# Hash attention and a maxout FFN on one core: sets of four heads placed by GpSimd instead of by transfers, with a new plan

## The chip, the cores and the metric

The kernel runs on one core of one Trainium2 chip. The metric is the device time of one execution in microseconds, the median of three runs. Engines: TensorE (PE for matmuls, PEld for its weight loads), VectorE (DVE), ScalarE (ACT), GpSimd (POOL), SyncE (SP, which here only issues DMAs). "A unit" is a step of the kernel's outer loop, explained below; it is the kernel's own clock.

## The reference

q, k and v have 4 batches of 8 heads of 768 tokens of 64 numbers; proj is 64x6. Each token falls in one of 64 buckets by the signs of six projections, and a query sees only keys of its own bucket:

```
q_bucket = sum((q @ proj > 0) * 2**arange(6));  k_bucket likewise
scores = where(q_bucket == k_bucket, q @ k.T / 8, -1e9)
attn = exp(scores - max) / (sum + 1e-9);  x = attn @ v      # heads side by side: 3072 x 512
h = max(x @ w1, x @ w2, x @ w3)                             # 512 -> 768
out = h @ w_out                                             # 768 -> 512, float32
```

## The kernel before, in words

**Masking by extra rows.** A head's S tile holds the 64 transposed numbers of its tokens (scaled, bf16) and under them six or eight rows of bits as +-0.5. The scores matmul over these 70 or 72 rows gives the scaled score plus a term that is at its maximum only where all bits agree; the exponential on ACT (L387) with its bias leaves the rest at almost nothing. No mask is ever formed.

**Units.** A unit is two blocks of 128 keys against one half (384) of a head's queries: two matmuls (L385) into PSUM, one exponential over 128x768 into one of the AT tiles (L387). There are 192 units; batch 0 is units 0 to 47 and takes heads two by two: pair 0 in units 0 to 11, pair 1 in 12 to 23, then the set of heads 4 to 7 in 24 to 47. Every later batch takes 48 units, 24 for each half of the queries.

**Getting S.** The heads come in three ways. Pair 0 and pair 1 are transposed by PE (L198), copied out of PSUM (L210), and GpSimd scales them into S (L217). Their bits come from PE hashes; for pair 0 VectorE writes them in place (L264), for pair 1 it writes a tile (L241) that SP's DMAs carry into S (L245). All other heads come in *sets* of four, one set for q and one for k for each g from 1 to 7, called q1, k1, ... q7, k7 here. `load_quad` (L277) loads one head into each 32 partitions, a DMA for each head. `turn` (L288) transposes 32x32 blocks on VectorE, four instructions a set. `narrow` (L295) scales to bf16 on GpSimd, two instructions a set, and `place` (L302) moves each head with a DMA on SP's queue to partitions 0 to 63 of the set's S tile. `quad_hash` (L312) and `quad_bits` (L318) make the bits of both sets of a g, and four DMAs on SP (L324) take them to S.

**The rest.** `values` (L431) multiplies AT with v for four heads at once, 24 matmuls a pass; `sums` (L445) adds up AT with a matmul of ones, for which, from unit 48 on (`adds`), VectorE first adds the AT tiles of a head (`gather`, three instructions a head: L413, L416, L418). `inverse` and `spread` (L452 to L460) turn sums into factors, `scale` (L464) writes the scaled result to the xT tiles. The FFN takes a half batch as 24 items: 18 groups of four matmuls (L545), of which ACT copies one and VectorE takes the maximum with two others (L551), then six items of the output matmul (L561). From unit 40 on one FFN item runs in each unit.

**Order.** Every engine executes in the order in which the program issues to it. Each step has a due time in units in PLAN; steps are sorted by it and issued when the loop passes it, which sets the order on each engine and on the DMA queues (SP, ACT, and GpSimd's own). A step with a negative time, or one whose time is earlier than the loop has reached, is issued as soon as it is seen, in order of those times. For g of 4 and more the times are offsets from the unit at which that g is first used. A step waits on its engine for its data and for free buffers: five load tiles (`nat`), three turned tiles (`t32`), 26 AT tiles.

The steps of the plan that come up below: `t` turns, `pl` placing, `l` loads of sets, `w` the eight half weights and `v` the values on GpSimd's queue, `p1t`/`p1k`/`p1h`/`p1b` transposes, copies, hashes and bits of pair 1, `h` hashes of sets, `q0` to `q6` and `q` the sums, values and scaling, `act` the copies that ACT makes, `last` the end.

Of the kernel before, what the change touches and what calls it, by code (L numbers as in the profile page):

```python
# [17 lines left out]
def kernel(  # L18
# [21 lines left out]
    Q = 32  # L40
# [11 lines left out]
    NAT = 26  # L52
# [31 lines left out]
        'adds': 48,  # L84
        'act': [(1, 0, 0), (3, 0, 1), (2, 1, 1), (2, 1, 0), (3, 1, 0), (1, 1, 1)],
        'last': ['F', 'A00', 'S', 'I', 'A10', 'A01', 'R0', 'R1', 'A11', 'X01', 'X10', 'X00', 'X11'],
        'ffn': [40, 53, 10],
        'skip': [],
        't1': [-45.57, -44.264, -44.181, -35.522],
        'pl1': -31.678,  # L90
        't0': [-37.547, -33.595, -26.867, -24.071],
        'pl0': -20.267,
        'l1': [-58.53, -72.053, -70.663, -68.669],
        'l0': [-59.075, -55.548, -56.26, -58.067],
        'vl': -20.089,
        'h': [-23.27, -23.26],
        'q': {'S': 0.71, 'I': 0.71, 'A00': 0.711, 'R0': 0.721, 'X00': 0.722, 'A01': 0.725, 'X01': 7.804, 'A10': 0.576, 'R1': 0.746, 'X10': 3.72, 'A11': 0.743, 'X11': 0.988},
        'fill': [8, 0, 0],
# [5 lines left out]
    t16_pool = ctx.enter_context(tc.tile_pool(name="t16", bufs=3))  # L104
# [8 lines left out]
    x_pool = ctx.enter_context(tc.tile_pool(name="xpool", bufs=3))  # L113
# [72 lines left out]

    def load_pair(pi, eng, sides=(1, 0), h0=0, h1=2):
# [48 lines left out]
    def pair_bits(pi, hds):  # L236
# [6 lines left out]
        for hd, side, n in gs:  # L243
            done.update(("bits", pi, 2 * side + hd, par) for par in range(2))
            nc.sync.dma_start(s_at(pi, 2 * side + hd, D, D + NBITS, 0, S).rearrange("b (c n) -> b c n", c=2),  # L245
# [23 lines left out]
    def load_quad(side, g, xs, eng):  # L269
        if (side, g) not in nat:  # L270
            start_set((side, g), [(side, 4 * g + x) for x in range(4)])
        for x in xs:
            done.add(("load", side, g, x))
            b, h = divmod(4 * g + x, H)
            src = (q, k)[side][b, h].rearrange("(cc t m) d -> t cc (m d)", cc=CC, t=Q)
            dst = nat[side, g][x * Q : (x + 1) * Q, :].rearrange("t (cc w) -> t cc w", cc=CC)
            eng.dma_start(dst, src)  # L277

    def turn(name, u, half):
        assert all(("load",) + name + (x,) in done for x in range(4))  # L280
# [9 lines left out]
    def narrow(name, u):  # L290
        if name not in t16:
            t16[name] = t16_pool.tile([P, 2, S], BF16, tag="T16", name="T16")
        assert {("turn", name, u, half) for half in range(2)} <= done
        done.add(("narrow", name, u))
        nc.gpsimd.tensor_scalar(out=t16[name][:, u, :], in0=t32[name][:, u, :], scalar1=RS, scalar2=1.0,  # L295
                                op0=AluOp.mult, op1=AluOp.mult)

    def place(name, xs):
        assert {("narrow", name, u) for u in range(2)} <= done
        for x in xs:  # L300
            done.update(("place", name, x, par) for par in range(2))
            nc.sync.dma_start(s_tile(name)[0:D, x, :], t16[name][x * Q : (x + 1) * Q, :, :])  # L302
# [486 lines left out]
```

## Time and profile before

| what | value |
|---|---|
| median of 3 runs | 273.28 us (270.22 to 274.68) |
| the profiled execution | 275.35 us, span 273.4 us |
| mean granted TensorE clock | 0.967 |
| PE busy | 256.5 us, 94% |
| VectorE busy | 196.4 us, 72% |
| ScalarE busy | 181.3 us, 66% |
| GpSimd busy | 62.8 us, 23% |
| moved by DMA | 31.76 MB, 22658 packets |

The span runs from the first to the last instruction of the profiled execution; all times in the views count from its start. Views that are used: the page's rows of busy tenths in 40 slices; the busy time of each engine in chosen stretches; the chain that ended last, followed back from the last instruction; the waits of an engine with what ended them; groups of instructions by line (line, engine, operation, out<-in, count, busy us, mean ns, idle before); and the timeline of single instructions (start, length, engine, line, and in brackets the idle time before it with what ended it).

### The profile page before, as it was taken

Reading aid. Unit: us, or ns where it says so; the run is one execution under the profiler, and the core shown is the slowest. Engines: PE = TensorE matmul, PEld = TensorE weight load, DVE = VectorE, ACT = ScalarE, POOL = GpSimd, SP = SyncE. Lnnn points to the kernel's source line nnn. Section 1 sums busy time; section 2 is a strip of 40 time slices with the busy share of each in tenths; the row PEclk is TensorE's granted clock in tenths of the full one; section 3 lists DMA queues with packets and bytes.
Section 4 is the critical chain, followed back from the end, with each engine's and each line's share of the span. In section 5 each row is a group of like instructions: output and inputs, shape, how many; then the busy total and the mean of one; then the engine's idle time right before and its main releaser. Section 6 shows DMA issues by size and latency. Waiting matters only on the chain.

```text
span 273.4 us, 5808 instructions
## 1 busy us (share of the span) xinstructions
PE 256.5 (94%) x2198; PEld 139.4 (51%) x2198; DVE 196.4 (72%) x450; ACT 181.3 (66%) x273; POOL 62.8 (23%) x102
## 2 busy tenths in 40 slices
PE   8864769999999999999999999999999999999995
PEld 4411223355555555555555555555555555555563
DVE  2753535675599789988898889987967887695350
ACT  3683374778399919993799648991999399911422
POOL 4275243913213332063016102202000000000000
PEclk9995895999999999999999999999999999999999
DMA  7999999899622732573356406324221001100303
GB/s 227 227 218 212 250 184 260 197 181 159 155 67 90 226 90 72 98 230 95 94 80 211 109 14 113 121 56 64 71 79 38 2 0 52 65 2 0 117 0 115
DMA packets 22658, 31.76 MB, mean 116 GB/s; under 512 B 2872, under 2 KB 18152, under 8 KB 22632
## 3 DMA queue, kind: packets, MB, share of 16 engines
q0 software_dynamic: 8704, 12.59, 24.5%
q1 hardware_dynamic: 13496, 18.30, 24.1%
q10 hardware_dynamic: 432, 0.52, 0.6%
q8 instruction: 17, 0.28, 0.4%
q14 instruction: 9, 0.07, 0.1%
HBM read 25.17 MB, written 6.29 MB: 115 GB/s over the span
## 4 chain that ended last, share of the span: by engine, by line
PE 80%; DMA 15%; SPq 2%; DVE 1%; issue 0%; POOL 0%; ACTq 0%; ACT 0%; DVEq 0%
PE ms L545 34%; PE sc L385 19%; PE ms L431 11%; PE ms L561 11%; DMA nat<-in_q_dram 8%; DMA S<-T 4%; PE ms L312 3%; DMA nat<-in_k_dram 3%; PE ms L445 2%; SPq L324 1%; PE ms L572 0%; SPq L302 0%; SPq L277 0%; POOL T L295 0%; DVE xT L464 0%
## 5 line engine op out<-in xcount | busy, mean ns | idle before, releaser
L387 ACT ACTIVATE AT<-sc 128x768 f16<-128x768 f32 x192 | 154.0, 828 | 62.3 <-PE sc L385 56.2
L545 PE MATMUL ms<-xT,w_sb 128*128 128x384 f16 x576 | 112.9, 326 | 0.4 <-DVE ht L551 0.4
L385 PE MATMUL sc<-S 72*128 72x384 bf16 (+1 forms) x360 | 88.7, 336 | 9.6 <-DMA S<-bits 7.0
L545 PEld LDWEIGHTS <-w_sb 128*128 128x128 f16 x576 | 55.9, 97 | 38.8 <-issue 0.9
L551 DVE TENSOR_TENSOR ht<-ht,ms 128x384 f16<-128x384 f16 x96 | 52.6, 547 | 27.2 <-PE ms L545 24.3
L385 PEld LDWEIGHTS <-S 72*128 72x128 bf16 (+1 forms) x384 | 36.4, 100 | 49.0 <-issue 21.5
L295 POOL TENSOR_SCALAR T<-T 128x768 bf16<-128x768 f32 x28 | 24.2, 864 | 113.4 <-DVE T L288 69.2
L431 PE MATMUL ms<-AT,vo 128*32 128x385 f16 (+1 forms) x768 | 36.4, 331 | 0.0
L561 PE MATMUL ms<-wout_sb,ht 128*128 128x512 f16 x138 | 36.0, 378 | 0.0
L549 ACT CAST ht<-ms 128x384 f16<-128x384 f32 x48 | 23.3, 486 | 16.2 <-DVE ht L551 10.3
L288 DVE STREAM_TRANSPOSE T<-nat 128x384 f32<-128x384 f32 x56 | 30.2, 559 | 3.4 <-DMA nat<-in_q_dram 3.3
L413 DVE TENSOR_TENSOR As<-AT,AT 128x768 f16<-128x768 f16 x48 | 27.9, 581 | 3.1 <-ACT AT L387 3.1
L416 DVE TENSOR_TENSOR As<-As,AT 128x768 f16<-128x768 f16 x48 | 27.2, 567 | 1.9 <-ACT AT L387 1.3
L431 PEld LDWEIGHTS <-vo 128*32 128x32 f16 x768 | 19.7, 97 | 14.8 <-issue 4.8
L464 DVE SCALAR_TENSOR_TENSOR xT<-ms,svs,rb 128x384 f16<-128x384 f32 (+1 forms) x36 | 21.8, 613 | 1.1
L561 PEld LDWEIGHTS <-ht 128*128 128x128 f16 x138 | 13.4, 97 | 12.8 <-DVE ht L551 0.6
L418 DVE TENSOR_TENSOR Ah<-As 128x384 f16<-128x384 f16 x48 | 17.7, 368 | 1.7
L565 ACT COPY osb<-ms 128x512 f32<-128x512 f32 x23 | 13.9, 604 | 6.5 <-PE ms L561 6.3
L318 DVE TENSOR_SCALAR bits<-ms 128x384 bf16<-128x384 f32 x7 | 3.9, 557 | 13.0 <-PE ms L312 13.0
L312 PE MATMUL ms<-T,pj 128*32 128x384 f32 x112 | 11.6, 537 | 0.6 <-DVE xT L464 0.6
L452 DVE STREAM_TRANSPOSE ys<-ms 128x384 f32<-128x384 f32 x10 | 5.8, 580 | 4.8 <-PE ms L445 4.8
L277 POOL DMA_DIRECT2D nat<-in_q_dram x16 | 9.2, 575 | 0.4
(60 smaller groups left out, 104.1 us busy)
## 6 DMA issues: line engine op xcount, KB each, us to landing
out_dram<-osb SPq DMA_DIRECT2D x23, 256.0 KB
S<-T SPq DMA_DIRECT2D x56, 96.0 KB
vo<-in_v_dram POOLq DMA_DIRECT2D x8, 384.0 KB, 5.7
nat<-in_k_dram POOLq DMA_DIRECT2D x16, 192.0 KB, 3.6
nat<-in_q_dram POOLq DMA_DIRECT2D x16, 192.0 KB, 4.8
nat<-in_k_dram SPq DMA_DIRECT2D x14, 192.0 KB
nat<-in_q_dram SPq DMA_DIRECT2D x12, 192.0 KB
w_sb<-in_moe_w_dram POOLq DMA_DIRECT2D x6, 384.0 KB, 8.0
```

Of the source, the lines that this page charges most:

```text
L288: nc.vector.transpose(t32[name][:, u, half * HALF : (half + 1) * HALF], i_)
L295: nc.gpsimd.tensor_scalar(out=t16[name][:, u, :], in0=t32[name][:, u, :], scalar1=RS, scalar2=1.0, op0=AluOp.mult, op1=AluOp.mult)
L385: nc.tensor.matmul(sc[:, j, 0:HALF], s_at(kn, kx, 0, D + nb, m * P, (m + 1) * P), s_at(qn, qx, 0, D + nb, qh * HALF, (qh + 1) * HALF), sta ...
L387: nc.scalar.activation(at_tiles[u % NAT][:, :, 0:HALF], sc[:, :, 0:HALF], ActFn.Exp, bias=-SCALE * 0.25 * nb, scale=SCALE)
L413: nc.vector.tensor_tensor(out=t[:], in0=at_tiles[(u - 1) % NAT][:, :, 0:HALF], in1=new, op=AluOp.add)
L416: nc.vector.tensor_tensor(out=t[:], in0=t[:], in1=new, op=AluOp.add)
L431: nc.tensor.matmul(av[r * Q : (r + 1) * Q, 0:cols], vt[:, x, c * D + s : (c + 1) * D : 2], at_of(g, m, hd)[:, 0:cols], start=(m == 0), sto ...
L464: nc.vector.scalar_tensor_tensor(out=o[o0 : o0 + p1 - p0, :], in0=av[p0:p1, 0:HALF], scalar=sv[p0:p1, :], in1=rc[p0:p1, :], op0=AluOp.add, ...
L545: nc.tensor.matmul(ps[:, 0:HALF], w_sb[wi][:, jc, fb * P : (fb + 1) * P], xt[:, jc, :], start=(jc == 0), stop=(jc == NJC - 1))
L549: nc.scalar.copy(hts[fb][:], ps[:, 0:HALF])
L551: nc.vector.tensor_tensor(out=hts[fb][:], in0=hts[fb][:], in1=ps[:, 0:HALF], op=AluOp.max)
L561: nc.tensor.matmul(ps[:, 0:DM], hts[fb][:, tb * P : (tb + 1) * P], wout_sb[:, fb, :], start=(fb == 0), stop=(fb == NFB - 1))
```

## The change

**Loads.** A set is now loaded with all four heads over the 128 partitions at once, 24 tokens in a row on each partition, in two DMAs that take half of the row each.

**Placing.** `narrow` is gone, and so are the DMAs of `place`. GpSimd writes S directly from the turned tile: for each head and each half of the 64 numbers one instruction from 32 partitions to 32 partitions over 768 elements, eight for a set, issued in two calls of two heads. The new token order on the partitions makes it write with a step of four elements. `quad_bits` writes its bits in the same order.

**Pair 1.** An option `p1m` lets pair 1 take the route of pair 0 for its bits, and `queue` lets chosen DMAs go by another engine's queue. With the numbers in this plan neither is in use: `p1m` is [0, 0], and no key of `eng` is one that is asked for. `straight` isn't called.

**Plan and buffers.** All due times are new. At the start, ten warm-up matmuls instead of eight stand ahead of the first transposes and five instead of eight behind them; PSUM's four shared banks are taken from the start. The four turns of k1, the transposes of pair 1's first q head and the loads w4, v1 and w5 have negative times, so they are issued right behind the first two units' scores. FFN items still begin at unit 40. AT has 28 tiles instead of 26, `t16` two instead of three, xT two instead of three. Among the last steps stand more FFN items.

```
-    NAT = 26
+    NAT = 28
-        'p1t': [1.347, 2.1, 4.1, 2.47],        'p1k': [2.11, 2.11, 4.12, 2.557],
-        'p1h': [4.344, 6.742],                 'p1b': [5.702, 12.812],
-        't11': [2.439, 6.495, 7.951, 8.3],     'pl11': 11.744,
-        't01': [11.333, 12.461, 7.712, 12.498], 'pl01': 17.924,
-        'w': [10.483, 11.72, 9.962, 19.928, 20.598, 22.093, 42.118, 38.918],
-        'v': [11.466, 38.572, 40.234],         'l': [6.2, 0.57, 20.339],
-        'ffn': [40, 53, 10],                   'fill': [8, 0, 0],
+        'p1t': [1.456, -24.099, 2.92, 3.224],  'p1k': [3.437, 0.435, 6.968, 5.811],
+        'p1h': [7.844, 9.742],                 'p1b': [10.418, 10.823],
+        't11': [-23.446, -5.508, -1.025, -57.408], 'pl11': [11.567, 3.727],
+        't01': [11.925, 10.905, 12.572, 10.935], 'pl01': [13.008, 13.018],
+        'w': [13.408, 15.206, 18.728, 12.088, -19.947, -0.356, 4.986, 46.113],
+        'v': [-4.428, 33.909, 35.556],         'l': [10.334, 13.929, 34.447],
+        'ffn': [40, 55, 15],                   'fill': [5, 0, 7, 10],
+        'pl12': [31.796, 32.611], 'pl02': [32.485, 31.427], 'pl13': [43.479, 43.465], 'pl03': [46.913, 47.473],
+        'pl1': [-28.093, -30.784], 'pl0': [-27.061, -25.566],
+        'p1m': [0, 0],  'eng': {('pl', 1, 1): 2, ('b', 2, 1): 2},
...
-    x_pool = ctx.enter_context(tc.tile_pool(name="xpool", bufs=3))
+    x_pool = ctx.enter_context(tc.tile_pool(name="xpool", bufs=2))
...
-    def load_quad(side, g, xs, eng):
+    def load_quad(side, g, part, eng):
...
-        for x in xs:
-            done.add(("load", side, g, x))
-            b, h = divmod(4 * g + x, H)
-            src = (q, k)[side][b, h].rearrange("(cc t m) d -> t cc (m d)", cc=CC, t=Q)
-            dst = nat[side, g][x * Q : (x + 1) * Q, :].rearrange("t (cc w) -> t cc w", cc=CC)
-            eng.dma_start(dst, src)
+        done.add(("load", side, g, part))
+        b, h = divmod(4 * g, H)
+        w = slice(part * 2 * HALF, (part + 1) * 2 * HALF)
+        eng.dma_start(nat[side, g][:, w], (q, k)[side][b, h : h + 4].rearrange("h (t w) d -> (h t) (w d)", t=Q)[:, w])
...
-    def narrow(name, u):
...
-        nc.gpsimd.tensor_scalar(out=t16[name][:, u, :], in0=t32[name][:, u, :], scalar1=RS, scalar2=1.0,
-                                op0=AluOp.mult, op1=AluOp.mult)
-    def place(name, xs):
...
-            nc.sync.dma_start(s_tile(name)[0:D, x, :], t16[name][x * Q : (x + 1) * Q, :, :])
+    def place(name, hp):
...
+        for x in (2 * hp, 2 * hp + 1):
+            done.update(("place", name, x, par) for par in range(2))
+            for u in range(2):
+                i_ = t32[name][x * Q : (x + 1) * Q, u, :].rearrange("p (m j t) -> p m j t", t=Q, j=CC)
+                o = s_tile(name)[u * Q : (u + 1) * Q, x, :].rearrange("p (m t j) -> p m j t", t=Q, j=CC)
+                nc.gpsimd.tensor_scalar(out=o, in0=i_, scalar1=RS, scalar2=1.0, op0=AluOp.mult, op1=AluOp.mult)
...
-        nc.vector.tensor_scalar(out=bits[:], in0=bp[:, 0:HALF], scalar1=0.0, scalar2=0.5,
+        nc.vector.tensor_scalar(out=bits.rearrange("p (m t j) -> p m j t", t=Q, j=CC),
+                                in0=bp[:, 0:HALF].rearrange("p (m j t) -> p m j t", t=Q, j=CC), scalar1=0.0, scalar2=0.5,
```

More of the change, by code (lines that the diff above doesn't have):

```diff
@@ L184, in s_at, with queue @@
         return s_tile(name)[p0:p1, x, lo:hi]
+    def queue(*key):
+        return (nc.sync, nc.scalar, nc.gpsimd)[PLAN["eng"].get(key, 0)]
     def load_pair(pi, eng, sides=(1, 0), h0=0, h1=2):
@@ L595 @@
         load_pair(1, nc.sync)
-        load_quad(1, 1, range(4), nc.sync)
-        load_quad(0, 1, range(4), nc.sync)
-        load_quad(1, 2, range(4), nc.sync)
+        for side, g in ((1, 1), (0, 1), (1, 2)):
+            for part in range(2):
+                load_quad(side, g, part, nc.sync)
         nc.gpsimd.memset(pj[:], 0.0)
@@ L614 @@
         bk, mk = [pool.tile([P, 512], FP32, name=n, tag=n) for n in ("bk", "mk")]
-        start = psum("start", bufs=1)
-        mq, bq, mk1, mq1 = [start.tile([P, 512], FP32, name=n, tag=n) for n in ("mq", "bq", "mk1", "mq1")]
+        phase(1)
+        mq, mk1, mq1, bq = [bank() for _ in range(4)]
         def fill(n, t, c=P):
@@ L686 @@
             for n, h in enumerate(hds):
-                when(T[f"p{pi}h"][n], pair_hash, pi, h)
-                when(T[f"p{pi}b"][n], pair_bits, pi, h)
+                near = pi == 1 and PLAN["p1m"][n]
+                when(T[f"p{pi}h"][n], *((head_hash, pi, n) if near else (pair_hash, pi, h)))
+                when(T[f"p{pi}b"][n], *((head_bits, pi, n) if near else (pair_bits, pi, h)))
         for n in range(8):
@@ L693 @@
         for n, (side, g) in enumerate(((0, 2), (1, 3), (0, 3))):
-            when(T["l"][n], load_quad, side, g, range(4), nc.sync)
+            for part in range(2):
+                when(T["l"][n], load_quad, side, g, part, nc.sync)
         def prepare(name, ts, tp):
@@ L698, in prepare @@
                 when(t, turn, name, n // 2, n % 2)
-                if n % 2:
-                    when(t + 0.01, narrow, name, n // 2)
-            when(tp, place, name, range(4))
+            for hp, t in enumerate(tp):
+                when(t, place, name, hp)
         for side, g in ((1, 1), (0, 1), (1, 2), (0, 2), (1, 3), (0, 3)):
@@ L710 @@
             for side in (1, 0):
[L711 to L713 removed]
+                prepare((side, g), [t0 + t for t in T[f"t{side}"]], [t0 + t for t in T[f"pl{side}"]])
+                for part in range(2):
+                    when(t0 + T[f"l{side}"][part], load_quad, side, g, part, nc.gpsimd)
             when(t0 + T["vl"], load_v, g)
```

52 lines of the change are left out of this document (24 added, 28 removed), and 54 rows, old and new, of the table PLAN.

## The prediction, made before the changed kernel ran

> **What bounds the kernel now.** I read the page first, then the busy time by stage, the chain, the waits, and the timelines of GpSimd (POOL), VectorE (DVE) and TensorE (PE).
>
> ```profile
> PE 256.5 (94%) x2198; PEld 139.4 (51%) x2198; DVE 196.4 (72%) x450; ACT 181.3 (66%) x273; POOL 62.8 (23%) x102
> PEclk9995895999999999999999999999999999999999
> DMA  7999999899622732573356406324221001100303
> ```
>
> 94% looks like a kernel with nothing left, but the clock row shows half speed in the fourth and sixth or seventh slice of 6.8 us: a busy PE there is a slow one. The stages, cut where the kernel itself cuts them (first exponential, unit 12, unit 24, unit 40 with the first FFN matmul, last matmul):
>
> ```profile
> 8.90:24.20 15.30, 8.56 (x51) 3.58 (x52) 9.10 (x18) 10.00 (x15) 10.15 (x18) 0.86 1.10 214
> 24.20:39.50 15.30, 11.04 (x88) 3.89 (x88) 5.92 (x12) 9.08 (x12) 5.80 (x8) 0.81 1.12 216
> 39.50:59.05 19.55, 18.86 (x220) 8.25 (x221) 11.43 (x28) 12.06 (x17) 8.72 (x13) 0.83 1.03 218
> 59.05:270.40 211.35, 210.91 (x1804) 119.71 (x1801) 166.21 (x356) 146.82 (x225) 35.04 (x49) 1.00 0.35 86
> ```
>
> The columns are stretch, length, then busy PE, PEld, DVE, ACT, POOL, the granted clock, DMA share, GB/s. From 59.05 us on PE is busy 210.91 of 211.35 us at full clock: nothing but less matmul work or a new wait changes that stage. All that can be won lies before 59.05 us, where the DMA share is about 1 and the clock 0.81 to 0.86.
>
> ```profile
> 16.62 7.22 DMA nat<-in_k_dram
> 23.85 8.10 DMA nat<-in_q_dram
> 34.20 5.23 DMA S<-T
> 52.27 1.50 PE ms L312 x16
> 54.53 1.09 PE ms L445 x24
> 55.62 0.98 PE ms L431 x24
> 56.60 0.76 PE sc L385 x4
> 59.21 0.65 PE ms L545 x4
> ```
>
> ```profile
> 24.19 1.44 PE L385 MATMUL sc<-S 70*128 70x384 bf16 x4 [5.22 <-DMA S<-bits]
> 26.62 2.79 PE L312 MATMUL ms<-T,pj 128*32 128x384 f32 x16
> 33.79 1.14 PE L385 MATMUL sc<-S 70*128 70x384 bf16 x6 [1.77 <-DMA S<-bits]
> 39.56 0.48 PE L385 MATMUL sc<-S 72*128 72x384 bf16 x2 [2.05 <-DMA S<-T]
> 34.31 4.43 ACT L387 ACTIVATE AT<-sc 128x768 f16<-128x768 f32 x6 [1.45 <-PE sc L385]
> ```
>
> The chain says the same in time: loads up to 31.97 us, then the transfer that places the first set (34.20 to 39.43 us), after which PE begins unit 24 at 39.56 us. Unit 12 had waited 5.22 us for bits of the second pair, whose small transfers stand on SP's queue behind set loads. The ACT row gives six exponentials, one a unit, in 4.43 us: 0.74 us each.
>
> **The change part by part.** *Transfers and loads.* Each of the 14 sets loses two narrowings and four SBUF transfers; its load becomes two DMAs over 128 partitions in place of four over 32.
>
> ```profile
> S<-T SPq DMA_DIRECT2D x56, 96.0 KB
> L295 POOL TENSOR_SCALAR T<-T 128x768 bf16<-128x768 f32 x28 | 24.2, 864 | 113.4 <-DVE T L288 69.2 <-issue 24.1 <-PE sc L385 10.4
> L217 POOL TENSOR_SCALAR S<-T 64x384 bf16<-64x384 f32 x13 | 6.6, 506 | 6.1 <-DVE T L210 5.1 <-ACT T L210 0.2
> L277 POOL DMA_DIRECT2D nat<-in_k_dram x16 | 9.0, 565 | 0.2
> ```
>
> *Placing.* A set takes eight GpSimd instructions of 32x768 instead. None is in the trace. L217 (384 elements, 64 partitions) takes 0.506 us, L295 (768, 128 partitions) 0.83 unhindered: the length follows the elements per partition, so I take 0.83 us, the lower bound; the upper is 1.06, what L295 takes when held by VectorE (two in 2.13 us, shown below). The unknown is the output, written with a step of four bf16 (8 bytes). So 112 x 0.83 = 93 us replace 24.2 us. A pair of sets costs 16 x 0.83 = 13.3 us of GpSimd in 24 units (29.3 us, 1.22 a unit); narrowing (3.5) and half of eight load issues (8 x 0.57 / 2 = 2.3) go, so GpSimd does not become the bound there.
>
> The GPSIMD Engine Reference of the Trainium skill (7. Performance pitfalls for Q7 kernels) has reads go from about 1.9 to 2.9 cycles an element when the step exceeds 8 bytes. Here the step is exactly 8, and on the output; by that rule 0.83 us holds at the very limit, and past it a place would take an estimated 0.83 x 2.9 / 1.9 = 1.27 us and make the slower rival below the likeliest. No run here shows a strided GpSimd instruction.
>
> *First stage, unit 0 to 12.* Two more warm-up matmuls stand ahead of the first transpose. The eight of now end as it begins, so they delay it by up to 2 x 0.34 = 0.7 us:
>
> ```profile
> 1.12 2.74 PE L619 MATMUL mq<-warm 128*128 128x384 f16 x8 [1.12 <-DVE pj L600]
> 3.92 0.88 PE L198 MATMUL mk<-iden,nat 128*128 128x128 f32 x3
> ```
>
> The four turns of the first k set now stand on VectorE ahead of everything of pair 0's second head and of pair 1; its load is the fifth and sixth 0.39 MB on SP's queue, and I expect it about 11 us, when VectorE is just through with the first head. Neither sets unit 12. That is set, as now, by the second pair's bits: the plan holds 'p1m': [0, 0], so the route in place by VectorE is not taken, no key of 'eng' matches, and the bits still go by SP. Ahead of them on that queue stand the pairs and the sets k1, q1, k2 and q2: 4.3 MB, as many as now (k1, q1, k2, k3).
>
> ```profile
> q1 hardware_dynamic: 1975, 2.66, 90.4%
> q0 software_dynamic: 475, 0.37, 19.9%
> ```
>
> These are 10 to 24 us: SP's queue has nearly all of the DMA engines. Three more GpSimd loads (w4, v1, w5), now issued from some 12 us, will take a part of it; what packets of twice the size give back no row shows. I take 24.2 us, unchanged, with 22 and 27 as bounds.
>
> *Unit 12 to 24, 15.3 us now.* The work is 12 units of scores (0.76 / 2 = 0.38, 4.6 us), one hash at the low clock (2.79) and three passes over the values (3 x 1.1): 10.7 us, 11.8 with the first scores at half clock; twelve exponentials at 0.74 (8.9) lie beside it. What must arrive: k1 and q1 placed. GpSimd is through with pair 0 as now and then issues w4, v1 and w5:
>
> ```profile
> 9.50 2.26 POOL L217 TENSOR_SCALAR S<-T 64x384 bf16<-64x384 f32 x4 [2.85 <-DVE T L210]
> L339 POOL DMA_DIRECT2D w_sb<-in_moe_w_dram x6 | 4.4, 738 | 0.2
> ```
>
> That is 11.8 + 3 x 0.74 = 14 us. Then it has pair 1 (8 x 0.506), 16 places (13.3) and two weight issues (1.5): 18.9 us, done at 33, ahead of unit 24 at 24.2 + 11.8 = 36.0. Bits of the set follow its hash at 28 us and one set's load; I expect them at 32. Gain 3.5 us (0 to 5).
>
> *Unit 24 to 40, 19.55 us now.* 16 units of scores (6.1), six passes (0.98 to 1.09, 6.2) and a hash (1.5 at full clock) are 13.8 us; ACT needs 16 x 0.74 = 11.8. With 0.7 for the alternation 14.5 us, so unit 40 at 50.5. The transfers that stopped PE here are gone, and the second stretch of low clock with them. w0 to w2, issued after q1's places (33.4 to 36), then have 14 us to land. Gain 5.05 us (0 to 6). Cover that is thin: q2 and k2 need 13.3 us of GpSimd from 40 us and turn buffers free for q3 at 53; q3's first half, after k3, would be ready at some 70 us for unit 60 at 75.
>
> *FFN stage: a new conflict.* VectorE's sums of AT (L413, L416, L418) start with unit 48 and read two SBUF tensors. The timeline shows what happens when GpSimd's L295 is running:
>
> ```profile
> 107.20 0.83 POOL L295 TENSOR_SCALAR T<-T 128x768 bf16<-128x768 f32 x1 [6.97 <-DVE T L288]
> 107.50 0.94 DVE L413 TENSOR_TENSOR As<-AT,AT 128x768 f16<-128x768 f16 x1
> 108.82 0.55 DVE L416 TENSOR_TENSOR As<-As,AT 128x768 f16<-128x768 f16 x1
> 109.41 0.36 DVE L418 TENSOR_TENSOR Ah<-As 128x384 f16<-128x384 f16 x1
> 174.18 0.52 DVE L413 TENSOR_TENSOR As<-AT,AT 128x768 f16<-128x768 f16 x1
> 174.35 2.13 POOL L295 TENSOR_SCALAR T<-T 128x768 bf16<-128x768 f32 x2 [6.89 <-DVE T L288]
> 175.10 0.69 DVE L416 TENSOR_TENSOR As<-As,AT 128x768 f16<-128x768 f16 x1
> 175.83 0.86 DVE L418 TENSOR_TENSOR Ah<-As 128x384 f16<-128x384 f16 x1
> 110.00:140.00 30.00, 30.00 (x264) 16.99 (x263) 26.91 (x58) 22.66 (x35) 8.80 (x13) 1.00 0.50 125
> ```
>
> Each waits until the other's instruction ends: L413 0.94 us instead of 0.55, L416 0.69 instead of 0.55, L418 0.86 instead of 0.36, and GpSimd's two take 2.13 instead of 1.7. So a head, with one of each, costs VectorE 0.39 + 0.14 + 0.50 = 1.03 us more while GpSimd places. The 13.3 us of a pair of sets, stretched by the sums, meet four heads of the eight in 24 units: 4.1 us, 0.6 of which I take as paid today by the four narrowings. VectorE is idle 3.1 of 30 us in the last row. Left over: 4.1 - 0.6 - 3.1 = 0.4 us, and about 0.3 because the burst (units 59 to 74) reaches the half's end, where sums are awaited: 0.7 a pair, 2.8 us for the four pairs placed in this stage (0 to 14).
>
> *Other edits.* Deeper AT (28), x_pool at 2 and the later FFN entry (55, 15) change no work: FFN items run one a unit from 40 on without a hole in either plan. The FFN items among the last steps fill a PE that has no gap now. The strided bits (7 instructions) are bounded by -0.1 and +0.3 us each, away from the path: 0.
>
> *Sum.* The profiled execution took 275.35 us, its span 273.4, 1.95 outside; the median is 273.28. Span: 273.4 - 3.5 - 5.05 + 2.8 = 267.65, that is 5.75 less. From the median: **267.5 us**.
>
> **The rivals.** *The queue eats the start.* w4, v1 and w5 share the engines from 12 us, bits land at 27, w0 to w2 wait behind 13.3 us of places, and only 2 of 8.55 us remain: 273.3 - 2 + 2.8 = 274. For it: SP's queue holds 90.4% today because nothing else asks. Against: the same bytes stand ahead of the bits.
>
> *Sums cost nothing.* PE's four PSUM banks take up VectorE's lag; 273.3 - 8.55 - 1 = 264. For it: PE has no idle to speak of with VectorE at 26.91 of 30. Against: VectorE is in order, and the FFN's L551 stands behind every held sum.
>
> *VectorE becomes the bound (slower).* If a place takes 1.06 us, each of a head's three sums waits up to 0.23 us longer (1.03 + 0.69 = 1.72), and 16 x 1.06 = 17 us of places, stretched by the sums, meet 5.5 heads: 9.5 - 3.7 (the 0.6 and 3.1 above) = 5.8 us lost in each of four pairs, 23 us: 273.3 - 8.55 + 23 = 288. It decides from 8.55 / 4 = 2.1 us lost a pair. For it: 26.91 of 30 leaves little room. Against: the rows hold sums 0.14 to 0.50 us, never a whole instruction.
>
> **How the numbers follow.** Forecast 0.37 (own range 264 to 270.5), queue 0.26, nothing lost 0.14, VectorE bound 0.23. About 2% (5.5 us) is what a measurement of this kernel can tell from no change: faster means below 267.8, slower above 278.7. Of the forecast 0.32 and all of "nothing lost" are faster, 0.46; the queue case and 0.05 are within, 0.31; slower is 0.23. The range leaves out the far half of the slower case and the best of the other: 260 to 283.
>
> **What would show it.** Right: no S<-T transfers; places of 0.83 us; unit 24 near 36 us and the first L545 near 50.5 us; one stretch of low clock fewer; L418 often near 0.86 us; PE idle on VectorE of 2 to 4 us after 60 us. Wrong: the first L545 after 55 us, places over 1.1 us, or VectorE busy above 29 of 30 us with PE waiting for ht.

## The result, and the profile after

The changed kernel takes **363.79 us** (median of four runs, 362.53 to 364.33) against 273.21 us before on the same chip: a ratio of 1.336, 95% interval 1.324 to 1.347. The forecast was 267.5 us, range 260 to 283. The profiled execution's span is 361.7 us, 88.3 more than before's 273.4. Executions of before fall into a faster and a slower state, and all ratios here compare executions in the faster one.

The page of the changed kernel (engines, then groups of instructions: busy us, mean ns of one):

```profile
PE 284.9 (79%) x2197; PEld 149.9 (41%) x2197; DVE 271.0 (75%) x452; ACT 182.8 (51%) x273; POOL 243.7 (67%) x170
L304 POOL TENSOR_SCALAR S<-T 32x768 bf16<-32x768 f32 x112 | 214.3, 1914 | 26.5 <-PE sc L388 18.0
...
L421 DVE TENSOR_TENSOR Ah<-As 128x384 f16<-128x384 f16 x48 | 48.5, 1011 | 1.7
...
L419 DVE TENSOR_TENSOR As<-As,AT 128x768 f16<-128x768 f16 x48 | 45.8, 954 | 2.9 <-ACT AT L390 2.6
L416 DVE TENSOR_TENSOR As<-AT,AT 128x768 f16<-128x768 f16 x48 | 44.6, 929 | 4.0 <-ACT AT L390 3.9
```

A place (L304) takes 1.914 us, not 0.83. VectorE's three sums of AT take about 1 us each. On the page of before they were shorter:

```profile
L413 DVE TENSOR_TENSOR As<-AT,AT 128x768 f16<-128x768 f16 x48 | 27.9, 581 | 3.1 <-ACT AT L387 3.1
L416 DVE TENSOR_TENSOR As<-As,AT 128x768 f16<-128x768 f16 x48 | 27.2, 567 | 1.9 <-ACT AT L387 1.3
L418 DVE TENSOR_TENSOR Ah<-As 128x384 f16<-128x384 f16 x48 | 17.7, 368 | 1.7
```

The sums take 48.5 + 45.8 + 44.6 = 138.9 us now and took 72.8: 66.1 us more of VectorE for the same work. The last two stages of the changed kernel, cut as before's were (columns: stretch, length, busy PE, PEld, DVE, ACT, POOL, clock, DMA share, GB/s):

```profile
39.99:66.84 26.85, 21.05 (x220) 8.67 (x220) 13.59 (x29) 12.89 (x18) 25.06 (x15) 0.75 0.35 65
66.84:358.30 291.46, 235.67 (x1802) 129.23 (x1802) 237.45 (x355) 147.49 (x223) 186.80 (x113) 0.89 0.20 54
...
140.00:170.00 30.00, 21.60 (x133) 11.41 (x126) 29.62 (x36) 19.53 (x29) 29.04 (x19) 1.00 0.33 96
...
290.00:320.00 30.00, 30.00 (x254) 17.05 (x253) 22.61 (x52) 24.01 (x38) 0.00 (x0) 1.00 0.10 36
```

Read against before's rows, the FFN stage takes 291.46 us in place of 211.35 (+80.1). It starts at 66.84 us in place of 59.05 (+7.8, nearly all of it behind unit 24: 26.85 us where before had 19.55). With 0.4 us at the tail that is the 88.3.

The last two rows are of 30 us each. From 140 us on GpSimd is busy for 29.04 of them and VectorE for 29.62, while TensorE, which was busy for all 30.00 in before's row from 110 to 140 us, is busy for 21.60. From 290 us on GpSimd has no work left, and TensorE is full.

TensorE's timeline gives the starts of unit 12, unit 24 and the pass behind it:

```profile
24.01 1.44 PE L388 MATMUL sc<-S 70*128 70x384 bf16 x4 [3.61 <-DMA S<-bits]
...
39.99 0.57 PE L388 MATMUL sc<-S 72*128 72x384 bf16 x2 [4.19 <-POOL S L304]
...
53.04 2.12 PE L434 MATMUL ms<-AT,vo 128*32 128x385 f16 x24 [4.33 <-DVE ys L455]
```

The waits (us in total, how often, the longest) are TensorE's largest in the FFN stage and then, over the whole span, VectorE's for GpSimd's places:

```profile
PE ms L548 <- DVE ht L554: 23.2, 11, 4.9
PE ms L448 <- DVE Ah L421: 15.8, 4, 4.0
PE sc L388 <- POOL S L304: 8.8, 3, 6.8
```

```profile
DVE T L291 <- POOL S L304: 15.7, 2, 8.4
```

Unit 12 comes as forecast (24.01 us). From unit 24 on, TensorE waits for S tiles from GpSimd or for VectorE's results. In the FFN stage it is idle for 55.8 us (291.46 less 235.67): 47.0 of them end with a result of VectorE (the first two rows and 8.0 us of smaller waits), 8.8 with an S tile. A part of the 47.0 is GpSimd's lateness by another way. VectorE stood twice before a transpose (the last row) until GpSimd's places had freed a turn buffer: for 7.4 us up to 51.8 us, and for 8.4 us up to 79.3 us. TensorE's longest wait for ht, 4.9 us, comes right behind the second.

TensorE was also busy for longer: 235.67 us in place of 210.91 for the same matmuls, at a granted clock of 0.89 in place of 1.00. So the 80.1 us are 55.4 more of idle time and 24.8 more of busy time. What lowers the clock was not tested. It was 0.77 from 170 to 200 us and 0.85 from 200 to 230, where TensorE was busy for 23.03 and 21.42 of 30 us, but 1.00 in the row from 140 us with about as little work.

### The profile page after: what moved, and what is told of

Read it like the earlier page. It is cut to its first block, busy times and chain, and to the rows that moved or that the text cites. A ratio compares the mean times of both kernels' runs of the same rounds, so it can differ in the third digit from the quotient of the medians.

```text
span 361.7 us, 5784 instructions
## 1 busy us (share of the span) xinstructions
PE 284.9 (79%) x2197; PEld 149.9 (41%) x2197; DVE 271.0 (75%) x452; ACT 182.8 (51%) x273; POOL 243.7 (67%) x170
## 4 chain that ended last, share of the span: by engine, by line
PE 45%; POOL 27%; DVE 20%; issue 6%; ACT 0%; POOLq 0%; DVEq 0%
POOL S L304 23%; PE ms L548 19%; PE sc L388 9%; PE ms L434 7%; PE ms L564 6%; DVE As L416 5%; DVE As L419 5%; DVE Ah L421 3%; DVE ht L554 3%; DVE T L291 2%; PE ms L314 2%; POOL S L222 2%; PE ms L622 1%; POOL vo L336 1%; POOL nat L280 1%
## 5 line engine op out<-in xcount | busy, mean ns | idle before, releaser
L304 POOL TENSOR_SCALAR S<-T 32x768 bf16<-32x768 f32 x112 | 214.3, 1914 | 26.5 <-PE sc L388 18.0
L548 PE MATMUL ms<-xT,w_sb 128*128 128x384 f16 x576 | 119.9, 340 | 25.6 <-DVE ht L554 23.2
L421 DVE TENSOR_TENSOR Ah<-As 128x384 f16<-128x384 f16 x48 | 48.5, 1011 | 1.7
L434 PE MATMUL ms<-AT,vo 128*32 128x385 f16 (+1 forms) x768 | 44.1, 372 | 6.8 <-DVE ys L455 4.3
L419 DVE TENSOR_TENSOR As<-As,AT 128x768 f16<-128x768 f16 x48 | 45.8, 954 | 2.9 <-ACT AT L390 2.6
L416 DVE TENSOR_TENSOR As<-AT,AT 128x768 f16<-128x768 f16 x48 | 44.6, 929 | 4.0 <-ACT AT L390 3.9
L291 DVE STREAM_TRANSPOSE T<-nat 128x384 f32<-128x384 f32 x56 | 30.2, 558 | 21.9 <-POOL S L304 15.7
L434 PEld LDWEIGHTS <-vo 128*32 128x32 f16 x768 | 24.1, 107 | 41.2 <-issue 29.7
L552 ACT CAST ht<-ms 128x384 f16<-128x384 f32 x48 | 23.3, 484 | 23.2 <-PE ms L548 12.6
L448 PE MATMUL ms<-Ah,pick 128*32 128x384 f16 x48 | 4.6, 331 | 15.8 <-DVE Ah L421 15.8
L314 PE MATMUL ms<-T,pj 128*32 128x384 f32 x112 | 16.2, 695 | 0.1
L463 DVE STREAM_TRANSPOSE rb<-rr 128x384 f32<-128x384 f32 x16 | 9.2, 577 | 0.2
```

What stands on the lines that cost most here:

```text
L291: nc.vector.transpose(t32[name][:, u, half * HALF : (half + 1) * HALF], i_)
L304: nc.gpsimd.tensor_scalar(out=o, in0=i_, scalar1=RS, scalar2=1.0, op0=AluOp.mult, op1=AluOp.mult)
L314: nc.tensor.matmul(bp[Q * r : Q * (r + 1), 0:HALF], pj[:, u, :], ts[side][:, u, j * HALF : (j + 1) * HALF], start=(u == 0), stop=(u == 1))
L416: nc.vector.tensor_tensor(out=t[:], in0=at_tiles[(u - 1) % NAT][:, :, 0:HALF], in1=new, op=AluOp.add)
L419: nc.vector.tensor_tensor(out=t[:], in0=t[:], in1=new, op=AluOp.add)
L421: nc.vector.tensor_tensor(out=z[:], in0=t[:, 0, :], in1=t[:, 1, :], op=AluOp.add)
```

## The experiments

The theory from the comparison has two parts. First, a place is 1.91 us long because of the step of its output, not because of its 32 partitions or its type. Second, while GpSimd runs places, VectorE's sums, which read two SBUF operands, are held up. The rivals are that GpSimd is slow on 32 partitions or is itself held by VectorE, and that late S tiles alone explain the loss.

**Forms of one instruction.** A kernel of nothing but GpSimd, VectorE and ScalarE instructions on SBUF tiles, four of each form on 768 elements a partition, then sums beside places and sums beside memsets.

> This kernel leaves out the whole computation: it runs GpSimd, VectorE and ScalarE instructions of several forms, four of each, and then GpSimd beside VectorE. In the changed kernel a place took 1.91 us where 0.83 was forecast. Theory A (the step of the output, four bf16, is the price): plain 32x768 takes 0.83 us, the form of the place 1.9, a plain step of 4 also 1.9, and 128 partitions make no difference. Theory B (32 partitions use a quarter of the engine, or a start on other partitions costs): plain 32x768 takes 1.9 too and 128x768 plain 0.83. Theory C (the walk over three dims is the price): the simple step of 4 takes 0.83, the place's form 1.9. Beside each other: sums wait for the places (up to 1.4 us each), and if only reading is shared they do not wait for memsets of the same shape.

Groups of its trace follow, one form after the other (the mean ns is the second number behind the bar; x3 where the view's window holds three of the four). In order: plain on 32 partitions, plain on 128, output step of two bf16, of four, of eight, the place's own pattern; then fp32 output with a step of two and of four, and fp32 input with a step of two and of four:

```profile
L48 POOL TENSOR_SCALAR dst<-src 32x768 bf16<-32x768 f32 x4 | 3.3, 821 | 5.6 <-DVE dst L53 5.3
...
L48 POOL TENSOR_SCALAR dst<-src 128x768 bf16<-128x768 f32 x4 | 3.3, 831 | 0.3
...
L48 POOL TENSOR_SCALAR dst<-src 32x768 bf16<-32x768 f32 x3 | 3.1, 1031 | 0.2
...
L48 POOL TENSOR_SCALAR dst<-src 32x768 bf16<-32x768 f32 x4 | 7.5, 1880 | 0.3
...
L48 POOL TENSOR_SCALAR dst<-src 32x768 bf16<-32x768 f32 x4 | 14.3, 3577 | 0.3
...
L48 POOL TENSOR_SCALAR dst<-src 32x768 bf16<-32x768 f32 x3 | 5.6, 1881 | 0.2
...
L48 POOL TENSOR_SCALAR dstf<-src 32x768 f32<-32x768 f32 x4 | 3.5, 864 | 0.3
...
L48 POOL TENSOR_SCALAR dstf<-src 32x768 f32<-32x768 f32 x4 | 6.1, 1535 | 0.3
...
L48 POOL TENSOR_SCALAR dst<-dstf 32x768 bf16<-32x768 f32 x4 | 3.4, 851 | 0.3
L48 POOL TENSOR_SCALAR dst<-dstf 32x768 bf16<-32x768 f32 x4 | 6.1, 1520 | 0.3
```

The partitions make no difference (0.821 and 0.831). The output's step does: 1.03, 1.88 and 3.58 us for two, four and eight bf16. The place's pattern, alone and with no VectorE beside it, takes 1.88. So the price is the write's. In the same trace stand six sums of 128x768 beside places (L84) and six beside memsets that write the same stepped pattern (L90):

```profile
L84 DVE TENSOR_TENSOR c<-a,b 128x768 f16<-128x768 f16 x6 | 10.6, 1775 | 0.2
...
L90 DVE TENSOR_TENSOR c<-a,b 128x768 f16<-128x768 f16 x6 | 3.8, 641 | 0.2
```

Beside places, which read and write, a sum lasts nearly as long as a place. Beside memsets of 1.79 us, which only write, it is 0.64, near the 0.55 of an undisturbed sum in before. So the hold goes with GpSimd's reading, and it costs a sum about 1.1 to 1.2 us; the places beside the sums take 1.94 us and are hardly held. (The Trainium skill, SBUF — State Buffer, section "SBUF: two separate sides", has this rule: a VectorE instruction with two SBUF inputs and a GpSimd instruction that reads SBUF lock each other out for a whole instruction. The two rows agree as far as VectorE's wait goes.)

**Places written plain.** The reordering of tokens is left out, so that places and bits are written without a step; all else as changed.

```
-                i_ = t32[name][...].rearrange("p (m j t) -> p m j t", t=Q, j=CC)
-                o = s_tile(name)[...].rearrange("p (m t j) -> p m j t", t=Q, j=CC)
+                i_ = t32[name][...]
+                o = s_tile(name)[...]
```

> The changed kernel with the places and the set bits written without a step (tokens of a set stay in the turned order, so keys meet the wrong rows of v: the reordering is left out). Nothing else differs. Theory A: a place takes 0.83 us, and everything else of the blind working is tested: first FFN matmul near 50.5 us, 264 to 270.5 us in all. Theory B: a place stays at 1.9 us and the time at 363 us. If places take 0.83 us and the time is still above 280 us, VectorE's waits in the FFN stage are the cause whatever the place's length.

Measured: 283.66 us, ratio 1.043 (1.036 to 1.050). Its page, two moments of TensorE's timeline, the stages behind unit 24 with one row of 30 us, and two of TensorE's waits:

```profile
L304 POOL TENSOR_SCALAR S<-T 32x768 bf16<-32x768 f32 x112 | 101.1, 902 | 55.9 <-PE sc L387 34.9
...
L418 DVE TENSOR_TENSOR As<-As,AT 128x768 f16<-128x768 f16 x48 | 32.1, 670 | 1.7 <-ACT AT L389 1.3
L415 DVE TENSOR_TENSOR As<-AT,AT 128x768 f16<-128x768 f16 x48 | 31.0, 646 | 2.3 <-ACT AT L389 2.2
...
L420 DVE TENSOR_TENSOR Ah<-As 128x384 f16<-128x384 f16 x48 | 28.2, 588 | 1.6
```

```profile
23.56 1.44 PE L387 MATMUL sc<-S 70*128 70x384 bf16 x4 [3.04 <-DMA S<-bits]
...
45.80 1.50 PE L314 MATMUL ms<-T,pj 128*32 128x384 f32 x16 [1.04 <-DVE xT L466]
```

```profile
36.21:52.91 16.70, 15.66 (x221) 7.38 (x221) 13.59 (x32) 13.07 (x19) 10.15 (x14) 1.00 0.55 105
52.91:277.30 224.39, 213.38 (x1803) 122.59 (x1801) 185.18 (x355) 147.41 (x225) 92.74 (x108) 1.00 0.25 71
110.00:140.00 30.00, 27.52 (x247) 16.11 (x245) 28.07 (x51) 20.10 (x32) 18.02 (x21) 1.00 0.33 96
```

```profile
PE ms L447 <- DVE Ah L420: 4.5, 4, 1.1
PE ms L547 <- DVE ht L553: 3.4, 5, 1.2
```

The stepped writes, of the places above all, are worth 363.79 - 283.66 = 80 us. The first stages now run as forecast within 2.4 us. But the kernel is still slower than before: the FFN stage is 13.0 us longer than before's 211.35, with sums of 91.3 us (+18.5 over before). TensorE is idle there for 11.0 us (224.39 less 213.38), and all of it ends with a result of VectorE: the two rows of waits and 3.1 us more for ht. None ends with an S tile from GpSimd, so late S tiles are no part of these 13.0 us.

**The step on the read side.** `rearrange("p (m j t) -> p m t j")` on the input, the output in order; the same reordering.

> The changed kernel with the reordering of the place moved from the output to the input: the output is written plain, the fp32 input is read with a step of 32 elements (128 bytes). Whole computation. Theory A (a step on the write alone is dear): 0.83 to 1.2 us a place and about 270 to 300 us. If any step is dear: 1.9 us or more a place and 360 us or more.

Measured once: 338.12 us, with places of 1.599 us, between the two outcomes expected. The far step costs a read about what a step of four cost in the forms (1.52). Moving it from one side of the instruction to the other gives back a third of the 80 us, no more.

**The far sets written by memsets.** For the sets of the last two batches (g >= 4) GpSimd runs a memset in the place's own pattern; q and k of those batches are left out.

```
+                if name[1] >= 4:
+                    nc.gpsimd.memset(s_tile(name)[...].rearrange("p (m t j) -> p m j t", t=Q, j=CC), 0.0)
+                    continue
```

> The changed kernel, in which the places of the sets of g of 4 and more are memsets of zeros to the same places with the same step: q and k of batches 2 and 3 are left out. A memset of this form takes 1.78 us alone, so GpSimd is as long busy as before, but reads nothing. Theory A (VectorE's sums are held while GpSimd reads): sums behind unit 96 take 0.55 to 0.6 us again, the four half batches that see these sets fall from some 42 us to 29.3 to 30 us, the whole to about 310 us. Theory B (GpSimd is late with S, or any busy GpSimd holds VectorE): 355 to 365 us, as the changed kernel.

Measured once: 317.31 us. Groups, TensorE's waits over the whole span, and the FFN stage:

```profile
L303 POOL MEMSET S<- 32x768 bf16 x64 | 116.4, 1819 | 2.7
...
L419 DVE TENSOR_TENSOR As<-AT,AT 128x768 f16<-128x768 f16 x48 | 30.3, 630 | 8.8 <-ACT AT L393 8.7
L422 DVE TENSOR_TENSOR As<-As,AT 128x768 f16<-128x768 f16 x48 | 30.0, 625 | 4.0 <-ACT AT L393 3.8
L424 DVE TENSOR_TENSOR Ah<-As 128x384 f16<-128x384 f16 x48 | 22.7, 472 | 1.7
```

```profile
PE sc L391 <- POOL S L307: 14.6, 5, 7.5
PE sc L391 <- POOL S L303: 5.4, 5, 3.4
```

```profile
66.83:312.15 245.32, 221.64 (x1802) 121.73 (x1802) 182.08 (x355) 147.60 (x223) 179.01 (x113) 0.95 0.23 65
```

GpSimd is about as busy as in the changed kernel (179 us in the stage, 187 there), with instructions about as long; their reading is gone. The sums fall from 138.9 to 83.0 us and the stage from 291.46 to 245.32. So 46 of the 80 us lost in the FFN stage are the hold between GpSimd's reading and VectorE's sums in the last two batches' sets. (A memset doesn't wait for a turned tile either, but in that stage of the changed kernel no wait of GpSimd ends with a transpose.) The other 34 can be read from the stage: TensorE waits 14.9 us for S tiles from GpSimd, 8.2 for VectorE's results and 0.6 for one of ScalarE's, and its matmuls take 10.7 us longer than before's at a granted clock of 0.95; before had 0.4 us of idle time. So late S tiles are a part of the changed kernel's loss, and the hold is the larger part.

**The far sets by transfers, places plain.** The places are plain, and the sets with g >= 4 go before's way: two narrowings over 128 partitions and four transfers by SP.

> The run with the plain write (the reordering of tokens left out), in which the sets of g of 4 and more are narrowed and moved by transfers. The plain write lost 13 us in the FFN stage. Theory A (16 places of 0.83 us a pair hold VectorE's sums): first FFN matmul at 53 us as there, the half batches back from 32.3 to 29.3 or 29.6 us, in all 270 to 273 us. Theory B (the new order of steps loses it): 282 to 284 us, no change.

Measured: 270.93 us, ratio 0.9987 (0.9951 to 1.0024). The FFN stage and the same 30 us:

```profile
53.15:265.34 212.19, 211.21 (x1804) 119.57 (x1801) 169.34 (x355) 146.92 (x224) 47.98 (x60) 1.00 0.35 90
110.00:140.00 30.00, 30.00 (x264) 16.88 (x262) 27.14 (x57) 22.77 (x36) 8.03 (x11) 1.00 0.52 128
```

With 16 narrowings in place of 64 places TensorE is full again. Its waits for VectorE in the stage fall from 11.0 to 1.0 us, and the sums take 76.7 us (91.3 with all places plain, 72.8 before). That settles the second part: even unstepped, eight places a set hold the sums enough to cost 13 us, and two narrowings of 128 partitions hardly do. The FFN stage begins 5.9 us earlier than in before's profile, yet the time is only level with before. That profile is of an execution of 275.35 us, while the executions of before that enter this ratio have a median of 271.5; where those gain their time was not profiled.

**Whole computations.** Three kernels compute everything: VectorE's transposes write the new order (an output step of four fp32), and the places are plain. The first moves no set by transfers, the second those with g >= 4, the third those with g >= 3.

```
-        nc.vector.transpose(t32[name][:, u, half * HALF : (half + 1) * HALF], i_)
+        nc.vector.transpose(t32[name][:, u, half * HALF : (half + 1) * HALF].rearrange("p (m t j) -> p m j t", t=Q, j=CC), i_)
```

> The changed kernel with the reordering moved from the place to VectorE's transposes: these write their fp32 output with a step of four elements (16 bytes), places and set bits are written plain. Whole computation. If a transposing instruction writes such a step at full rate it stays at 0.56 us and the time is that of the plain write, 282 to 285 us; if a step costs VectorE as it costs GpSimd (1.5 us), 56 of them add 50 us of VectorE and the time is over 310 us.

> As the one before, but only the sets of g of 1 to 3 are placed by GpSimd; the sets of g of 4 and more are narrowed and moved by transfers as in the kernel before. Whole computation. Theory A (16 plain places a pair hold VectorE's sums and cost PE 3 us in each of four half batches): first FFN matmul at 53 us as with the plain write, and then 211 to 214 us as in the kernel before: 268 to 272 us. Theory B (the plan's new order or the smaller buffers lose the 13 us of the FFN stage): no gain over 283 us.

> As the one before with the sets of g = 3 by transfers too, whose places fall into units 48 to 60, where the first sums stand. Theory A: 0 to 2 us faster than the one before. If their transfers come too late for unit 60: slower by 1 to 5 us.

Measured: 292.62 us (ratio 1.079, 1.070 to 1.087), 281.0 (1.036, 1.028 to 1.043) and 278.06 (1.027, 1.020 to 1.033). The transposes of the first one:

```profile
L291 DVE STREAM_TRANSPOSE T<-nat 128x384 f32<-128x384 f32 x56 | 46.0, 863 | 1.5 <-DMA nat<-in_k_dram 1.4
```

One takes 0.863 us, between the two outcomes expected, where the plain one takes 0.558 (30.2 us for 56 in the changed kernel): 15.8 us more on VectorE, the engine that has no room. The plain kernel and the first of these differ in the transposes' output alone, and between them the FFN stage's start moves from 52.91 to 57.08 us and the time from 283.66 to 292.62. In the third kernel the FFN stage is down to 214.4 us, but it starts only at 58.62; what of that late start is the transposes' was not separated.

**The new form of the loads, undone.** The plain places with before's loads, one DMA for each head over 32 partitions, rows of 1536 B.

> As the one before, but with the loads of the kernel before (a head on 32 partitions by a DMA of its own, four DMAs a set), for which no reordering is needed: the whole computation is there. It tells what the form of the loads is worth: if larger rows and fewer DMAs matter, it is 2 to 5 us slower than the run before; by my working (bytes set the arrival, not their form) it is within 2 us of it.

Measured: 288.76 us, 1.063 (1.054 to 1.073). Unit 12 of this kernel:

```profile
28.96 1.44 PE L389 MATMUL sc<-S 70*128 70x384 bf16 x4 [4.49 <-DMA S<-bits]
```

Unit 12 comes 5.4 us later than with the new loads (23.56), the FFN stage 5.8 us later (58.72 against 52.91). So the new form of the loads, which I had held for worth nothing, is worth five microseconds. Up to unit 12 the rest of the new start costs nearly as many: with the old loads unit 12 comes 4.8 us later than before's 24.19. The next kernels ask what in the form does it.

**Other rows.** With twelve tokens of each half on a partition the transposes write with a step of two, which costs them nothing (0.562 us measured). The load then has the four heads as its outermost dimension. The second kernel of this kind has only the first sets (g = 1) placed by GpSimd; the third is the first with a DMA of its own for each head, over 32 partitions. A fourth kernel is the plain one with far transfers (270.93 us above), but with each set loaded by four DMAs over all 128 partitions, with rows of 1536 B.

```
+        src = (q, k)[side][b, h : h + 4, part * HALF : (part + 1) * HALF].rearrange("h (t w) d -> h t (w d)", t=Q)
```

```
+        for c in (2 * part, 2 * part + 1):
+            w = slice(c * HALF, (c + 1) * HALF)
+            eng.dma_start(nat[side, g][:, w], (q, k)[side][b, h : h + 4].rearrange("h (t w) d -> (h t) (w d)", t=Q)[:, w])
```

> Whole computation. Loads still with 3072 bytes a row over 128 partitions, but of 12 tokens in a row from each half of the head, so that only a step of two is left to put in order, which VectorE's transposes write (8 bytes in fp32; the step of four, 16 bytes, took them from 0.56 to 0.86 us). Sets of g = 1 and 2 placed by GpSimd with a plain write, g of 3 and more by transfers. If a step of 8 bytes costs the transposes nothing, as it cost GpSimd's fp32 write 0.04 us: first FFN matmul at 53 to 55 us, then 211 to 213 us, 268 to 271 us in all, under the kernel before. If it costs them half of what the step of four does: 273 to 275 us.

> As the one before, with only g = 1 placed by GpSimd and g = 2 by transfers too. If GpSimd's places of g = 2 cost nothing before unit 48: the same within 1 us. If they delay loads that stand behind them on GpSimd's queue: 1 to 3 us faster.

> The whole computation. The edit of w3_half_rows once more (rows of 3072 B, two for each partition and head, twelve tokens of each half; the turns write with a step of two, the places are plain, sets from the fourth on are moved by transfers), but each set is loaded by one DMA for each head, four to a set, so that a DMA's slowest dimension has 32 entries and not the four heads. Theory A, w3 lost its time because a DMA whose slowest dimension is four heads keeps only a few of the core's DMA engines at work: the DMAs of the stretch from 2 to 24 us move 280 to 300 GB/s again (186 in w3_half_rows, 292 in after), first matmul of the FFN stage at 53 to 57 us (89.19 in w3_half_rows), total 266 to 273, so 0.975 to 1.0 of before. Theory B, two rows of 3072 B for a partition and head are slow by themselves, or the order of the queue does it: first matmul of the FFN stage at 75 or later, total 300 or more.

> The edit of e7_plain_far_transfer (places and bits written plain, sets from the fifth on moved by transfers; the reordering of tokens is left out), with each set loaded by four DMAs over all 128 partitions with rows of 1536 B, where e7_plain_far_transfer has two with rows of 3072 B. It tells what made the new loads worth about 5 us at the start. Theory A, it is that one DMA goes over all 128 partitions: the stretch from 2 to 24 us still moves 280 to 300 GB/s, first matmul of the FFN stage at 52.5 to 55, total 270 to 273, within 1% of e7_plain_far_transfer's 270.93. Theory B, it is the length of the rows: 240 to 260 GB/s as in before and e2_old_loads, first matmul of the FFN stage at 57 to 60, total 275 to 279.

Measured: 321.71 us (1.187, 1.181 to 1.194), 323.38 (1.193, 1.185 to 1.202), 279.29 (1.025, 1.019 to 1.032) and 273.46 (1.004, 0.999 to 1.010). The second is no faster than the first. This is what the DMAs of the first did from 24 to 58 us, in 40 slices (share of the 16 engines in tenths), while TensorE waited 28.1 us for bits queued behind its loads:

```profile
DMA  2222229697222389942222268999999422222222
```

For most of this time about a quarter of the DMA engines' time is used. (The Trainium skill, DMA: Bandwidth & Descriptors, section "Why a DMA increments its semaphore by 16 and not by 1", has a DMA use the largest number of engines up to 16 that divides its patterns' slowest dimensions; four heads give four of 16, and the 2s in the row agree.) With one DMA a head the first matmul of the FFN stage came at 58.22 us, not 89.19: most of that loss was this, though the speed stayed below the 280 to 300 GB/s I expected. The DMAs from 2 to 24 us, in this order: the plain places with new loads, the same with old loads, the last two kernels above:

```profile
DMA packets 4166, 6.49 MB, mean 295 GB/s; under 512 B 380, under 2 KB 3141, under 8 KB 4165
```

```profile
DMA packets 4616, 5.64 MB, mean 256 GB/s; under 512 B 443, under 2 KB 4616, under 8 KB 4616
```

```profile
DMA packets 3340, 5.30 MB, mean 241 GB/s; under 512 B 424, under 2 KB 2427, under 8 KB 3340
```

```profile
DMA packets 5241, 6.41 MB, mean 291 GB/s; under 512 B 497, under 2 KB 5241, under 8 KB 5241
```

The start of unit 12 in the last of them:

```profile
26.11 1.44 PE L395 MATMUL sc<-S 70*128 70x384 bf16 x4 [3.03 <-DMA S<-bits]
```

Over 128 partitions the start moves 295 and 291 GB/s with rows of 3072 and 1536 B; over 32 partitions it moves 241 and 256, again with either row. So the speed goes with the partitions that one DMA covers. The times say that this is not all. Unit 12 comes at 23.61 us with long rows in two DMAs a set (the 270.93 us kernel), at 26.11 with short rows in four, and at 28.96 with short rows in four over 32 partitions; the FFN stage begins at 53.15, 54.51 and 58.72. So the partitions are worth 2.9 us at unit 12 and 4.2 at the FFN stage; 2.5 and 1.4 us go with the longer rows or the smaller number of DMAs, which no run separates. In the whole time the ratio with short rows is 0.6% higher, with intervals that overlap. (The Trainium skill, SBUF — State Buffer, subsection "Door 1", has 32 neighbouring partitions reach only eight of the 16 DMA ports. The rows agree in sign; they mix loads of several forms and cannot show the ports.)

## Why the prediction was wrong, point by point

*The price of a place*: this step failed. I wrote "the length follows the elements per partition, so I take 0.83 us, the lower bound; the upper is 1.06". The rule holds for plain instructions (0.821 and 0.831 us on 32 and 128 partitions), but the step of the output, which I named as the unknown, more than doubles it: 1.88 alone, 1.914 in the kernel. The term of 112 x 0.83 = 93 us measured 214.3. The upper bound came from a row without a step and so bounded nothing of the unknown. A bf16 write pays at four bytes already (1.03) and 2.3 times at eight. (The rule of the Trainium skill that the prediction cites, GPSIMD Engine Reference, section "7. Performance pitfalls for Q7 kernels", is on reads and has its limit beyond eight bytes. The fp32 reads agree with that limit, 0.851 at 8 bytes and 1.520 at 16, though not with its price: 1.520 is 1.85 times the plain 0.82, not about 1.5 times (2.9 / 1.9). Taking it over to writes made 1.27 us look like the worst case.)

*Unit 12 at 24.2*: measured 24.01, but the reason was half wrong. That "the same bytes stand ahead of the bits" was not enough: with the old loads and the new plan (and plain places) unit 12 came at 28.96, worse than the 27 of the queue rival. The new loads paid it back. Two terms of about five microseconds each, which I had netted at nothing, cancelled; that the number came out was luck. The two more warm-up matmuls put the first transposes at 4.30 us in place of 3.92, within the 0.7 allowed, and the bits did go by SP's queue (the 3.61 us of unit 12).

*Unit 24 at 36.0, unit 40 at 50.5*: in the changed kernel 39.99 and 66.84. Unit 24 waited 4.19 us for the first places of q1's set. GpSimd was with that set until 51.8, and VectorE, whose next transpose needed a turn buffer, stood 7.4 us until then; TensorE's 4.33 us for ys lie behind that. The prediction had named turn buffers as a thin cover, for the next sets and at places of 0.83 us. With plain places the two came at 36.21 and 52.91, so the working was about right, given its price, with some luck at unit 24: that stretch began 0.6 us early and lasted 12.65 us where I had 11.8. The 2.4 us over at unit 40 are 0.2 carried from unit 24, a seventh pass of 24 matmuls where I counted six (five over the values and two sums; 1.1), and 1.04 of waiting for xT ahead of the hash. The granted clock was 1.00 in that stretch with plain places, as forecast, and 0.75 in the changed kernel.

*FFN stage, 2.8 us*: the second step that failed, apart from the price. With places of 0.90 us it lost 13.0. The hold itself was about right: 1.03 us for four heads in each of four pairs is 16.5 us, less 2.4 paid before, 14.1; the sums took 18.5 more. Wrong was to subtract VectorE's idle 3.1 us of 30. In the plain kernel's row from 110 to 140 us VectorE has 1.9 us idle and TensorE still loses 2.5: idle time elsewhere in a stretch does not take up a lag that TensorE waits for now. In the changed kernel the same stage also lost what I had put at nothing: 8.8 us of waits for S tiles, and matmuls 24.8 us longer at a lower granted clock. Without the subtraction the step gives 14 us and the sum about 279 even at 0.83 us a place.

*Strided bits, -0.1 to +0.3 us each*: the seven instructions took 1.017 us on average, against 0.556 with the plain write. The +0.46 is out of the bounds; it is 3.2 us in all, on VectorE.

*The rivals*: "VectorE becomes the bound" named the mechanism and the row to look at (VectorE busy for over 29 of 30 us with TensorE waiting for ht; measured 29.62, and 23.2 us of such waits in the stage), but was priced at 288 us from a place of 1.06. "Sums cost nothing" is refuted by the plain places, "the queue eats the start" by unit 12 in this kernel. All three warning signs that I gave came true: places over 1.1 us, the first FFN matmul after 55, and that row of VectorE.

The ledger: 363.8 less 283.7 with plain places is 80 us for the stepped writes. 283.7 less the forecast 267.5 is 16: 10.2 of it is the FFN stage beyond the 2.8 forecast, 2.4 the start. Nearly all of the rest is that the plain kernel's median lies 3.1 us above its profiled span, where the forecast stood at its span.

## What to carry to other kernels

Price a stepped write by a run of that very form, on that engine: a row for a plain instruction is no upper bound, and a rule for reads need not hold for writes. Where two engines hold each other up, count the held time against the wait that ends last there, not against the idle share of a window. Many small instructions can hold more than a few wide ones: here 64 places cost 13 us that 16 narrowings did not. When a reordering saves transfers, compare its cost on a full engine with the transfers' cost on queues that stand idle: with the far transfers back, TensorE was busy for 30.00 of 30 us.

## What the hardware showed beyond expectation

For 768 elements on GpSimd a bf16 write costs 0.82, 1.03, 1.88 and 3.58 us at a step of 1, 2, 4 and 8 elements, an fp32 write 0.82, 0.86 and 1.53 us at 1, 2 and 4: at 8 bytes fp32 is nearly free, bf16 is not. The place's pattern costs the other engines about twice the plain write too: ScalarE 1.90 in place of 0.84 us, VectorE 1.01 in place of 0.55. VectorE's transpose in fp32 is free at a step of two (0.562 us) and not at four (0.863). Set loads over 128 partitions bring the start to 288 to 297 GB/s, over 32 to 240 to 256. Loads with four heads outermost left about three quarters of the DMA engines' time unused.
